# A searched table of due times for the opening part of a fused attention and feed-forward kernel

## The chip, the cores and the metric

One core of one Trainium2 chip runs the program. TensorE (PE; its weight loads appear as PEld), VectorE (DVE), ScalarE (ACT), GpSimd (POOL) and SyncE (SP, which here only issues DMAs) each work through their own instruction list in order and wait for one another by semaphores. The metric is the device time of one execution in microseconds (us).

## The reference

Causal attention over 8 batches, 8 heads, 576 tokens of 64 channels, followed by a feed-forward layer:

```
scores = q @ k^T / 8
heads 0..3: keep key s for query t where 0 <= t - s < 32        (local)
heads 4..7: keep key s <= t where s % 32 == t % 32              (strided)
attn = softmax(scores) @ v ;  x = attn as 4608 tokens x 512
out = gelu(x @ w_in) @ w_out          (w_in 512 x 2048, w_out 2048 x 512)
```

## The kernel before

The 4608 tokens are cut into 9 tiles (`t`) of 512 tokens, and the 2048 hidden channels into 16 slices (`f`) of 128. One **pass** is one `f` of one tile: `H` is 12 matmuls of x with a slice of w_in into a PSUM bank, ACT then computes gelu and the copy `gh` (lines 767, 768), DVE the remainder `gl` (line 770), and `O` is 12 matmuls with a slice of w_out (line 779; H is line 741). Every fp32 operand is held as a high part and a low part, so each product takes three matmuls. TensorE's list is fixed: H of pass n, then O of pass n-1, then H of n+1, and so on. In tile 0 the slices f0 and f1 are done in two half passes each (pass numbers n = 0 to 3), so f2 is pass 4 and f15 is pass 17; H of pass 18 is the first of tile 1. Between passes the fixed list has the local scores of the next tile, `S` (line 425, behind f4 in tile 0), and its local values, `V` (line 466, behind the O of f12).

What the other engines do for this:

- **Weights**, once per f, all in tile 0: `load` (SP, 1 MB), then `lead` (ACT, line 332), `ws` (ACT, 333), `or` (DVE, 335), `hi` (ACT or DVE, 344) and `lo` (line 349, POOL for f > 2, DVE for f0 to f2). H of f needs hi and lo.
- **Local heads**: S on TensorE, `max` on DVE (485), `exp` on ACT (492), `quo` (504), `tr` (transpose, DVE 508), then V. For tile 1 on, `send` (SP, line 455) copies the transposed pieces, 4 pieces of 8 DMAs, ahead of V.
- **Strided heads**: products on POOL (and DVE at the start), sums on DVE, exp on ACT; names `oq`/`ov` for the first two tiles' rows, `q`/`v` later. `xl`, `xs` are x's local and strided halves, each split into h and l.

The order on every engine comes out of a list scheduler in the kernel, `Plan`: each step (`Op`) has candidate engines with a guessed duration and a due time, either given (`fixed`) or worked back from the step's users in `latest`; whenever an engine is free in the plan, the ready step with the earliest due time goes next. The plan's times are not on the chip: only the resulting order of each engine, and its choice of engine, are. The 17 slots of tag `w` hold weights and the opening's data in turn; a load waits until its slot is free.

Of the kernel before, what the change touches and what calls it, by code (L numbers as in the profile page):

```python
# [86 lines left out]
class Op:  # L87
    def __init__(self, eng, fn, deps, due, bufs, table, kb, name, rel, port, fixed):
        self.eng, self.fn, self.deps, self.due, self.bufs = eng, fn, deps, due, bufs
        self.table, self.kb, self.name, self.rel = table, kb, name, rel  # L90
        self.start = self.end = self.last = None
        self.port, self.fixed = port, fixed


class Plan:
# [19 lines left out]
    def run(self, busy):  # L115
        free = dict(busy)
# [7 lines left out]
        nxt, now, state, dma = 0, 0.0, "e", 0.0  # L124
# [33 lines left out]
        port = 0.0  # L158
        h_end = 0.0
        while count < len(self.ops):  # L160
            moved = False
            for e in free:
                if free[e] > now + 1e-9:
                    continue
                best = None
                for op in waiting[e]:
                    if at[op] > now + 1e-9:
                        continue
                    if e == "PE" and op not in self.floating and op is not self.pe[nxt]:
                        continue  # L170
                    if best is not None and op.due >= best.due:
# [73 lines left out]
def attn_ffn_kernel(ctx: ExitStack, tc: tile.TileContext, qk, qk0, vl, vl0, q0, k0, v0, q1, k1, v1, qs, ks, vs, w, out):  # L245
# [54 lines left out]
    def gps(n):  # L300
        return 0.33 + n * 0.00205
# [15 lines left out]
    def weights(f):  # L317
# [33 lines left out]
        o5 = plan.add({"POOL": 2.4} if f > HALVES else {"DVE": 1.25}, lo, [o4], due - 2, [raw, wt], name=f"lo{f}", port=True)  # L351
# [27 lines left out]
    def local(t):  # L379
# [26 lines left out]
        for j in range(NJ):  # L406
# [22 lines left out]
            s_ops[t, j] = plan.add({"PE": 0.4}, score if t else score0, [ld[j]], 0, [lq] + sb[j], name=f"S{t}.{j}")  # L429
# [4 lines left out]
        def after(o, pt, j, due):  # L434
            if t == 0:
# [10 lines left out]
                v_ops[t, j] = plan.add({"PE": 0.65}, value, [o, vo[j // 2]], 0, [vb, pt] + xb[j // 2], name=f"V{t}.{j}")  # L446
            else:
# [8 lines left out]
                o = plan.add({"SP": 4.4}, send, [o], due, [pt, bt], kb=1400, name=f"send{t}.{j}")  # L456
# [12 lines left out]
                v_ops[t, j] = plan.add({"PE": 0.45}, value, [o, vo], 0, [vb, bt] + xb, name=f"V{t}.{j}")  # L469

        for j in range(NJ):
# [37 lines left out]
            o = plan.add({"DVE": 0.7}, first, pair, due - 3, [pt, both] + sb[j], name=f"max{t}.{j}")  # L509
            o = plan.add({"ACT": 1.4}, second, [o], due - 2.5, [pt, both], table="e", name=f"exp{t}.{j}")  # L510
# [41 lines left out]
    def finish(t, sc, shape, deps, due, name):  # L552
# [58 lines left out]
    def unit(t, u, b, r0, nr, row, due):  # L611
# [33 lines left out]
        for i in range(nr):  # L645
# [11 lines left out]
            om = times(n * D, mul, [o, vlo], due - 2, [vb, sc, p], f"pv{name}.{i}")  # L657
# [65 lines left out]
    def ffn(t, wts):  # L723
# [4 lines left out]
        for f, c0, c1 in todo:  # L728
# [5 lines left out]
            MM = N / 2400.0 + 0.0127  # L734
# [222 lines left out]
```

## Time and profile before

| what | value |
|---|---|
| device time, 3 runs | median 881.13 us (880.54 to 881.37) |
| profiled execution | 880.88 us, span 879.0 us (1.9 us lie outside the span) |
| TensorE matmul busy | 838.0 us, 95% of the span |
| ACT, DVE, POOL busy | 410.1, 443.1, 503.4 us |
| mean granted TensorE clock | 0.991 of full speed |

Busy times are of the profiled execution; waits are read from the times at which instructions start.

### The profile page before, as it was taken

The numbers are of one execution on the slowest core, as the hardware profiler recorded it, in microseconds if no ns is written. First come the engines' busy times: TensorE is split into PE (matmuls) and PEld (weight loads), VectorE is DVE, ScalarE is ACT, GpSimd is POOL, SyncE is SP. The second block draws the span as 40 slices with busy tenths as digits, with TensorE's granted clock in tenths as the row PEclk, the third lists the DMA queues.
The fourth block names the chain that finished last, engine by engine and source line by source line (L and its number), as shares of the span: only waits on it lengthen the run. The fifth ranks groups of instructions, "written<-read, shape, count | busy, mean of one in ns | idle before, by whom it ended". The sixth has DMA issues, their size and how long they took to land.

```text
span 879.0 us, 15285 instructions
## 1 busy us (share of the span) xinstructions
PE 838.0 (95%) x5878; PEld 690.5 (79%) x5878; DVE 443.1 (50%) x946; ACT 410.1 (47%) x868; POOL 503.4 (57%) x433
## 2 busy tenths in 40 slices
PE   2798978999999999999999999999999999999997
PEld 1686756888888888888888888888888888888886
DVE  5877746755564655455545547356465651121111
ACT  4789934644454435434553346335623363222222
POOL 2567878876666874865576759477387760000000
PEclk9999988999999999999999999999999999999999
DMA  9928133110330113012211211111210310000001
GB/s 346 385 79 332 60 122 91 58 45 3 120 116 22 48 61 125 24 49 88 86 31 53 88 48 63 59 66 70 101 48 1 109 51 23 1 37 12 1 1 48
DMA packets 27672, 69.67 MB, mean 79 GB/s; under 512 B 5968, under 2 KB 14160, under 8 KB 25296
## 3 DMA queue, kind: packets, MB, share of 16 engines
q1 hardware_dynamic: 27600, 68.70, 22.0%
q8 instruction: 46, 0.75, 0.3%
q14 instruction: 26, 0.21, 0.1%
HBM read 55.05 MB, written 9.44 MB: 73 GB/s over the span
## 4 chain that ended last, share of the span: by engine, by line
PE 84%; ACT 6%; DMA 4%; DVE 2%; SPq 2%; issue 1%; POOL 0%; ACTq 0%
PE banks L741 41%; PE banks L779 40%; DMA w_raw<-in_w_dram 3%; PE banks L466 2%; DVE w_raw L335 2%; SPq L455 2%; ACT lead L332 1%; PE banks L425 1%; ACT w_raw L333 1%; DMA w_kv<-in_v_dram 1%; ACT pt L492 1%; ACT w_wt L344 1%; ACT L492 1%; ACT L767 1%; ACT banks L767 1%
## 5 line engine op out<-in xcount | busy, mean ns | idle before, releaser
L779 PE MATMUL banks<-w_wt,gh 128*128 128x512 f32 x1152 | 355.0, 389 | 0.3 <-ACT gh L768 0.3
L767 ACT ACTIVATE banks<-banks 128x512 f32<-128x512 f32 (+1 forms) x146 | 84.2, 577 | 386.6 <-PE banks L741 386.2
L779 PEld LDWEIGHTS banks<-w_wt,gh 128*128 128x128 f32 x1152 | 216.2, 188 | 45.3 <-ACT gh L768 0.7
L770 DVE TENSOR_TENSOR gl<-banks,gh 128x512 fp32r<-128x512 f32 (+1 forms) x146 | 99.5, 682 | 277.9 <-ACT gh L768 275.5
L779 PE MATMUL banks<-w_wt,gl 128*128 128x512 f32 x576 | 224.4, 390 | 0.8 <-DVE gl L770 0.8
L741 PE MATMUL banks<-xsh,w_wt 128*128 128x512 f32 (+1 forms) x584 | 162.5, 398 | 12.3 <-ACT w_wt L344 5.4
L741 PE MATMUL banks<-xlh,w_wt 128*128 128x512 f32 (+1 forms) x584 | 157.8, 391 | 0.6 <-ACT xlh L366 0.6
L741 PEld LDWEIGHTS banks<-xsh,w_wt 128*128 128x128 f32 x584 | 109.2, 191 | 38.0 <-POOL w_wt L349 6.8
L741 PEld LDWEIGHTS banks<-xlh,w_wt 128*128 128x128 f32 x584 | 111.1, 191 | 23.7 <-ACT xlh L366 0.8
L779 PEld LDWEIGHTS banks<-w_wt,gl 128*128 128x128 f32 x576 | 108.1, 188 | 24.0 <-DVE gl L770 1.7
L741 PE MATMUL banks<-xsl,w_wt 128*128 128x512 f32 (+1 forms) x292 | 91.1, 392 | 0.0
L741 PE MATMUL banks<-xll,w_wt 128*128 128x512 f32 (+1 forms) x292 | 90.5, 389 | 0.0
L768 ACT CAST gh<-banks 128x512 fp32r<-128x512 f32 (+1 forms) x146 | 84.9, 581 | 4.6
L741 PEld LDWEIGHTS banks<-xsl,w_wt 128*128 128x128 f32 x292 | 55.8, 192 | 11.6
L741 PEld LDWEIGHTS banks<-xll,w_wt 128*128 128x128 f32 x292 | 55.4, 190 | 11.6 <-DVE xll L371 0.2
L767 ACT ACT_TABLE_LOAD x38 | 48.8, 1283 | 0.7
L492 ACT ACTIVATE pt<-pt,lsm 128x64 f32<-128x64 f32 x128 | 42.8, 336 | 5.0 <-DVE lsm L485 4.8
L349 POOL TENSOR_TENSOR w_wt<-w_raw,w_wt 128x1024 fp32r<-128x1024 f32 x13 | 32.1, 2472 | 21.1 <-ACT w_wt L344 11.6
L504 POOL TENSOR_TENSOR pt<-pt,lsm 128x256 f32<-128x256 f32 x32 | 21.0, 676 | 26.1 <-DVE lsm L500 12.2
L335 DVE SCALAR_TENSOR_TENSOR w_raw<-w_raw 128x1024 uint32<-128x1024 uint32 x16 | 31.1, 1952 | 4.1 <-ACT w_raw L333 3.8
L585 ACT ACT_TABLE_LOAD x24 | 30.8, 1283 | 0.4
L466 PEld LDWEIGHTS banks<-bt,lq_v 64*64 64x64 f32 x1024 | 20.2, 134 | 7.1 <-issue 3.9
(900 smaller groups left out, 1026.1 us busy)
## 6 DMA issues: line engine op xcount, KB each, us to landing
w_raw<-in_w_dram SPq DMA_DIRECT2D x16, 1023.8 KB, 11.8
lq_qk<-in_qk_dram SPq DMA_DIRECT2D x8, 1280.0 KB, 5.9
lq_v<-in_vl_dram SPq DMA_DIRECT2D x8, 1024.0 KB, 5.2
out_dram<-w_ob SPq DMA_DIRECT2D x24, 256.0 KB, 2.3
sk<-in_ks_dram SPq DMA_DIRECT2D x8, 576.0 KB, 3.8
sv<-in_vs_dram SPq DMA_DIRECT2D x8, 576.0 KB, 3.9
bt<-pt SPq DMA_DIRECT2D x256, 16.0 KB, 1.8
sq<-in_qs_dram SPq DMA_DIRECT2D x8, 448.0 KB, 4.5
```

The lines of the kernel that those rows point to most:

```text
L335: o3 = plan.add({"DVE": 1.25}, lambda e: V.scalar_tensor_tensor(views["word"], views["word"], 13, views["other"], ALU.logical_shift_right, ...
L349: (V if e == "DVE" else G).tensor_tensor(views["t"][:, 1, :], views["word"].bitcast(F32), views["t"][:, 0, :].bitcast(F32), ALU.subtract)
L455: nc.sync.dma_start(bv[d:d + QB, a, :], pv[quarter(g), c, :])
L466: nc.tensor.matmul(xb[b]()[half(i), c:c + QB], vv[half(b), a, 2 * r + i, :], bv[half(b), a, 2 * r + i, :], start=True, stop=True, tile_pos ...
L492: A.activation(pv[:, :, h, :], pt()[:, 256 + h * 64:256 + (h + 1) * 64].rearrange("p (c t) -> p c t", c=2), AF.Exp, bias=sm[0]()[:, h:h + ...
L504: (V if e == "DVE" else G).tensor_tensor(pv, pv, sm[2]().unsqueeze(1).unsqueeze(3).to_broadcast([P, 2, HL, QB]), ALU.mult)
L585: o = plan.add({"ACT": act(n * c)}, lambda e: A.activation(view(), view(), AF.Exp, scale=SC), [o], due - 0.4, [sc], table="e", name=f"sexp ...
L741: nc.tensor.matmul(hp()[:, 0:c1 - c0], w1[f][:, lw, c, :], rx, start=((c, part) == (2, 0)), stop=((c, part) == end))
L767: A.activation(hp()[:, 0:N], hp()[:, 0:N], AF.Gelu)
L768: A.copy(a_()[:, 0:N], hp()[:, 0:N])
L770: o3 = plan.add({"DVE": dve(N)}, lambda e, hp=hp, a_=a_, b_=b_, N=N: V.tensor_tensor(b_()[:, 0:N], hp()[:, 0:N], a_()[:, 0:N].bitcast(F32) ...
L779: nc.tensor.matmul(o, x()[:, sl], w2[f][:, y, :], start=(f == 0 and i == 0), stop=(f == NF - 1 and i == 2))
```

## The change

A table `ORDER` of some 500 entries is added, one per named step of the opening and of the first tiles. For a step in it the due time is replaced by the table's, and a letter behind the number (V, A, G for DVE, ACT, POOL) also fixes the engine. The table was found by a search over the kernel's own scheduler. The scheduler's guessed durations and latencies are replaced by others, `lo` and `quo` may go to either POOL or DVE, gelu and gl get an earlier due time (`urgent`), and from planned time 140 on a step is not started on ACT or DVE just ahead of an expected gelu or gl. TensorE's list and the arithmetic stay as they were.

```diff
+URGENT = 20.0, 100.0
+STEADY = 140.0
+ORDER = """
+qk00:13.89 qk01:25.62 vl00:158.2 vl01:161.77 max0.0:-4534.87 exp0.0:-2303.89 max0.1:-4558.19
...
-    LAT = 0.08
+    LAT = 0.05
+    PE_LAT = 0.2
+    LAP = 0.05
...
         for op in reversed(self.ops):
-            op.due = op.due if op.fixed else latest(op)
+            op.due = op.due if op.fixed else round(latest(op) - op.urgent, 2)
+            if op.name in self.given:
+                op.due, e = self.given[op.name]
+                if e in op.eng:
+                    op.eng = {e: op.eng[e]}
...
+                    if now > self.steady and op.urgent == 0.0:
+                        if e == "ACT" and now - 0.19 < h_end < now + op.eng[e] - 0.5 + (
+                                1.3 * ((op.table == "e") + (state == "g")) if op.table or state == "e" else 0.0):
+                            continue
+                        if e == "DVE" and now - 0.04 < g_end < now + op.eng[e] - 0.4:
+                            continue
...
-                    dma = max(dma, now + 1.6) + op.kb / 370.0
-                    op.end = dma + 1.0
+                    dma = max(dma, now + 1.6) + op.kb / (230.0 if sent < 512 else 120.0 if sent < 1024 else 410.0)
+                    sent += op.kb
+                    op.end = max(dma + 0.6, free[e] + 1.2)
...
-        o5 = plan.add({"POOL": 2.4} if f > HALVES else {"DVE": 1.25}, lo, [o4], due - 2, [raw, wt], name=f"lo{f}", port=True)
+        o5 = plan.add({"POOL": 2.45, "DVE": 1.25}, lo, [o4], due - 2, [raw, wt], name=f"lo{f}", port=True)
...
-                o = plan.add({"SP": 4.4}, send, [o], due, [pt, bt], kb=1400, name=f"send{t}.{j}")
+                o = plan.add({"SP": 4.95}, send, [o], due, [pt, bt], kb=128, name=f"send{t}.{j}")
...
+            o2.urgent = o3.urgent = URGENT[n > 24]
...
+    plan.steady = STEADY
+    for x in ORDER.split():
+        name, due = x.split(":")
+        e = {"V": "DVE", "A": "ACT", "G": "POOL"}.get(due[-1])
+        plan.given[name] = float(due[:-1] if e else due), e
     todo = plan.run({"PE": 1.0, "DVE": 0.3, "ACT": 1.5, "POOL": 3.0, "SP": 0.0})
```

What it does to the lists, at three places. First SP, the first twelve loads (`q01`, `kv0`: strided inputs, `qk0`, `vl0`: the two halves of the local inputs, `raw0`, `raw1`: weights of f0 and f1). Before:

```order
L833 DMA w_q01_140<-in_q0_dram 128x512
L833 DMA w_kv0_142<-in_k0_dram 128x512
L386 DMA lq_qk0_144<-in_qk0_dram 128x1024
L325 DMA w_raw0_146<-in_w_dram 128x4095
L833 DMA w_kv0_142<-in_v0_dram 128x512
L397 DMA w_vl0_149<-in_vl0_dram 128x1024
L833 DMA w_q01_140<-in_q0_dram 128x512
L833 DMA w_kv0_142<-in_k0_dram 128x512
L386 DMA lq_qk0_144<-in_qk0_dram 128x1024
L325 DMA w_raw1_160<-in_w_dram 128x4095
L833 DMA w_kv0_142<-in_v0_dram 128x512
L397 DMA w_vl0_149<-in_vl0_dram 128x1024
```

The same place on SP after the change:

```order
L921 DMA w_kv0_140<-in_k0_dram 128x512
L473 DMA lq_qk0_142<-in_qk0_dram 128x1024
L921 DMA w_q01_144<-in_q0_dram 128x512
L473 DMA lq_qk0_142<-in_qk0_dram 128x1024
L921 DMA w_kv0_140<-in_k0_dram 128x512
L921 DMA w_q01_144<-in_q0_dram 128x512
L484 DMA w_vl0_149<-in_vl0_dram 128x1024
L412 DMA w_raw0_155<-in_w_dram 128x4095
L484 DMA w_vl0_149<-in_vl0_dram 128x1024
L921 DMA w_kv0_140<-in_v0_dram 128x512
L412 DMA w_raw1_159<-in_w_dram 128x4095
L921 DMA w_kv0_140<-in_v0_dram 128x512
```

The second half of qk0 has moved from ninth to fourth, and raw0 from fourth to eighth. Behind these stood raw2, the inputs k1, q1, v1 of the strided part of tile 1, raw3, raw4, qk1 (the local input of tile 1) and raw5; now raw2, q1, v1, k1, qk1, raw3, raw4, raw5. The lists of POOL then have the products oq1.0.0, oq1.0.1 and oq1.1.1, which read k1, ahead of the lo of f2, and oq1.1.0 behind it.

Second SP again, at the sends of tile 1 (`bt` is what V reads, `pt_1_j` the four transposed pieces). Before:

```order
L325 DMA w_raw12_943<-in_w_dram 128x4095
L325 DMA w_raw13_985<-in_w_dram 128x4095
L325 DMA w_raw14_1032<-in_w_dram 128x4095
L455 DMA bt_1_1053<-pt_1_0_732 32x128 x8
L455 DMA bt_1_1053<-pt_1_1_740 32x128 x8
L455 DMA bt_1_1053<-pt_1_2_763 32x128 x8
L455 DMA bt_1_1053<-pt_1_3_769 32x128 x8
L325 DMA w_raw15_1232<-in_w_dram 128x4095
```

The same place after the change:

```order
L412 DMA w_raw12_935<-in_w_dram 128x4095
L542 DMA bt_1_966<-pt_1_0_734 32x128 x8
L412 DMA w_raw13_1011<-in_w_dram 128x4095
L542 DMA bt_1_966<-pt_1_1_743 32x128 x8
L412 DMA w_raw14_1067<-in_w_dram 128x4095
L412 DMA w_raw15_1084<-in_w_dram 128x4095
L542 DMA bt_1_966<-pt_1_2_748 32x128 x8
L542 DMA bt_1_966<-pt_1_3_761 32x128 x8
```

raw15 has moved ahead of the last two sends, and raw13 and raw14 behind the first and the second.

Third DVE, from the gl of pass 9 (f7) to that of pass 10. Before:

```order
L770 TENSOR_TENSOR gl_9_909<-banks_71,gh_9_887 128x512
L638 TENSOR_REDUCE sc_2.0_871<-prod_q2.0.3_884 128x8
L638 TENSOR_REDUCE sc_2.0_871<-prod_q2.0.2_911 128x7
L638 TENSOR_REDUCE sc_2.0_871<-prod_q2.0.1_919 128x6
L770 TENSOR_TENSOR gl_10_939<-banks_71,gh_10_935 128x512
```

The same place after the change:

```order
L857 TENSOR_TENSOR gl_9_873<-banks_71,gh_9_858 128x512
L798 TENSOR_REDUCE w_acc1_820<-prod_ovo1.0.1_850 128x4x64
L422 SCALAR_TENSOR_TENSOR w_raw9_769<-w_raw9_769 128x1024
L798 TENSOR_REDUCE w_acc1_820<-prod_ovo1.0.0_877 128x4x64
L682 STREAM_TRANSPOSE w_acc1_820<-w_acc1_820 128x512
L431 CAST w_wt9_918<-w_raw9_769 128x1024
L587 RECIPROCAL lsm_1_0_735<-lsm_1_0_735 128x8
L436 TENSOR_TENSOR w_wt9_918<-w_raw9_769,w_wt9_918 128x1024
L591 TENSOR_TENSOR pt_1_0_734<-pt_1_0_734,lsm_1_0_735 128x256
L422 SCALAR_TENSOR_TENSOR w_raw10_797<-w_raw10_797 128x1024
L857 TENSOR_TENSOR gl_10_953<-banks_71,gh_10_925 128x512
```

DVE now has the lo of f9 here (L436), which stood on POOL; over the whole tile DVE has 13 of the 16 lo steps, where it had 3, and POOL has those of f2, f6 and f7. The strided work of tile 2 (prod_q2) has moved behind. On ACT the order of exp steps changes too: up to H of pass 18 its list has 12 table loads in place of 16, and behind it 92 in place of 60, since most exp steps of a tile now stand one by one between two gelus.

## Rows read from the trace of the kernel before

**Rows 1.** The page's first line: the span.
```profile
span 879.0 us, 15285 instructions
```
**Rows 2.** Windows: stretch, its us, each engine's busy us, granted clock, DMA share, GB/s.
```profile
0.00:10.00 10.00, 2.60 (x126) 2.32 (x126) 3.13 (x13) 1.49 (x2) 1.75 (x14) 1.00 0.78 252
10.00:40.00 30.00, 15.66 (x274) 13.60 (x275) 24.58 (x72) 23.44 (x62) 16.57 (x16) 1.00 1.02 424
90.00:100.00 10.00, 10.00 (x46) 8.19 (x45) 6.84 (x8) 9.90 (x19) 8.76 (x7) 1.00 0.30 106
120.00:130.00 10.00, 8.75 (x40) 6.74 (x40) 2.76 (x3) 2.85 (x4) 4.06 (x2) 0.68 0.64 241
150.00:200.00 50.00, 50.00 (x342) 41.26 (x342) 29.60 (x78) 27.34 (x68) 39.63 (x38) 1.00 0.22 63
```
**Rows 3.** Timeline of PE: start, us, instruction, count, idle time before and its releaser.
```profile
25.49 1.20 PE L741 MATMUL banks<-xsh,w_wt 128*128 128x256 f32 x4 [2.44 <-ACT w_pt L492]
...
47.78 1.07 PE L741 MATMUL banks<-xsh,w_wt 128*128 128x512 f32 x4
...
58.75 1.49 PE L425 MATMUL banks<-lq_qk 64*32 64x64 f32 x128
...
114.71 2.07 PE L466 MATMUL banks<-bt,lq_v 64*64 64x32 f32 x100
...
136.91 1.65 PE L741 MATMUL banks<-xsh,w_wt 128*128 128x512 f32 x3 [1.69 <-POOL w_wt L349]
...
143.70 1.07 PE L741 MATMUL banks<-xsh,w_wt 128*128 128x512 f32 x4
...
149.14 1.07 PE L741 MATMUL banks<-xsh,w_wt 128*128 128x512 f32 x4
...
221.63 2.53 PE L466 MATMUL banks<-bt,lq_v 64*64 64x32 f32 x128
```
**Rows 4.** Timeline of SP: the four sends of tile 1, and the load behind them.
```profile
98.66 21.56 SPq L455 DMA_DIRECT2D bt<-pt  x32
120.33 0.52 SPq L325 DMA_DIRECT2D w_raw<-in_w_dram  x1
```
**Rows 5.** Timeline of PE and ACT: first users of qk0's second half and of raw1.
```profile
15.79 1.13 PE L413 MATMUL banks<-lq_qk 64*64 64x64 f32 x32 [6.03 <-DMA lq_qk<-in_qk_dram]
18.22 1.11 ACT L332 CAST lead<-w_raw 128x1024 f16<-128x1024 bf16 x1 [2.06 <-DMA w_raw<-in_w_dram]
```
**Rows 6.** The tile w_raw: line, engine, count, duration in ns (min/median/max), first and last start.
```profile
L332 ACT CAST lead<-w_raw x16: 1073/1123/1203, 11.4 to 128.2; 128x1024 f16<-128x1024 bf16 x16
L333 ACT ACTIVATE w_raw<-lead x16: 1107/1131/1172, 12.5 to 129.3; 128x1024 int32<-128x1024 int16 x16
L335 DVE SCALAR_TENSOR_TENSOR w_raw<-w_raw x16: 1175/1662/3455, 13.7 to 130.5; 128x1024 uint32<-128x1024 uint32 x16
L349 POOL TENSOR_TENSOR w_wt<-w_raw,w_wt x13: 2403/2438/2894, 44.7 to 134.5; 128x1024 fp32r<-128x1024 f32 x13
L349 DVE TENSOR_TENSOR w_wt<-w_raw,w_wt x3: 1211/1219/1225, 16.1 to 43.6; 128x1024 fp32r<-128x1024 f32 x3
```
**Rows 7.** Timeline of DVE: an or that ran beside a lo on POOL.
```profile
44.77 3.46 DVE L335 SCALAR_TENSOR_TENSOR w_raw<-w_raw 128x1024 uint32<-128x1024 uint32 x1
```
**Rows 8.** The page's DMA issues: KB each, us to landing.
```profile
bt<-pt SPq DMA_DIRECT2D x256, 16.0 KB, 1.8
```
**Rows 9.** Timeline of ACT: the table load between exp and gelu, a gelu, its copy.
```profile
169.98 1.28 ACT L767 ACT_TABLE_LOAD   x1
171.27 0.58 ACT L767 ACTIVATE banks<-banks 128x512 f32<-128x512 f32 x1
171.88 0.59 ACT L768 CAST gh<-banks 128x512 fp32r<-128x512 f32 x1
```
**Rows 10.** The page's groups: gl, and the exp instructions, count, busy us, mean ns.
```profile
L770 DVE TENSOR_TENSOR gl<-banks,gh 128x512 fp32r<-128x512 f32 (+1 forms) x146 | 99.5, 682 | 277.9 <-ACT gh L768 275.5
L492 ACT ACTIVATE pt<-pt,lsm 128x64 f32<-128x64 f32 x128 | 42.8, 336 | 5.0 <-DVE lsm L485 4.8
```

More of the change, by code (lines that the diff above doesn't have):

```diff
@@ L36, in order_of_rows @@
+sq3.1.3:289.03 smax3.1:274.63
+"""
 def order_of_rows(nb, nr):
@@ L103, in __init__ @@
         self.floating = set()
+        self.given = {}
+        self.steady = 1e9
     def add(self, eng, fn, deps=(), due=0.0, bufs=(), table=None, kb=0, name="", rel=None, port=False, fixed=False):
@@ L123, in run @@
         waiting = {e: [] for e in free}
-        nxt, now, state, dma = 0, 0.0, "e", 0.0
+        nxt, now, state, dma, sent = 0, 0.0, "e", 0.0, 0.0
         after = dict(zip(self.pe, self.pe[1:]))
@@ L145, in offer @@
         def offer(op):
-            at[op] = max([d.end + self.LAT for d in op.deps] + [op.rel])
+            at[op] = max([d.end + (self.PE_LAT if d.engine == "PE" else self.LAT) for d in op.deps] + [op.rel])
             for e in op.eng:
@@ L158, in run @@
         port = 0.0
-        h_end = 0.0
+        h_end = g_end = 0.0
         while count < len(self.ops):
@@ L199, in run @@
                 op.start, op.engine = now, e
-                free[e] = now + dur
                 op.end = now + dur
+                free[e] = op.end - (self.LAP if e in ("DVE", "ACT", "POOL") else 0.0)
                 if op.port and e in ("DVE", "POOL"):
@@ L207, in run @@
                         h_end = op.end
+                if op.table == "g":
+                    g_end = op.end
                 if op.kb:
-                    dma = max(dma, now + 1.6) + op.kb / 370.0
-                    op.end = dma + 1.0
+                    dma = max(dma, now + 1.6) + op.kb / (230.0 if sent < 512 else 120.0 if sent < 1024 else 410.0)
+                    sent += op.kb
+                    op.end = max(dma + 0.6, free[e] + 1.2)
                 tick += 1
@@ L508, in fifth @@
                 V.transpose(pt()[:, 256:512], pt()[:, 0:256])
-            o = plan.add({"DVE": 0.7}, first, pair, due - 3, [pt, both] + sb[j], name=f"max{t}.{j}")
-            o = plan.add({"ACT": 1.4}, second, [o], due - 2.5, [pt, both], table="e", name=f"exp{t}.{j}")
+            o = plan.add({"DVE": 0.66}, first, pair, due - 3, [pt, both] + sb[j], name=f"max{t}.{j}")
+            o = plan.add({"ACT": 1.37}, second, [o], due - 2.5, [pt, both], table="e", name=f"exp{t}.{j}")
             exps.append((o, fourth, fifth, pt, j, due))
@@ L516, in local @@
             for o, fourth, fifth, pt, j, due in exps:
-                o = plan.add({"POOL": 0.75} if t else {"POOL": 0.75, "DVE": 0.46}, fourth, [rec], due - 1.5, [pt, both], name=f"quo{t}.{j}", port=True)
+                o = plan.add({"POOL": 0.65, "DVE": 0.46} if t < 2 else {"POOL": 0.65}, fourth, [rec], due - 1.5, [pt, both], name=f"quo{t}.{j}", port=True)
                 o = plan.add({"DVE": 0.46}, fifth, [o], due - 1, [pt], name=f"tr{t}.{j}")
@@ L579, in seventh @@
             (V if e == "DVE" else G).tensor_tensor(view(), view(), wide(m()[:, 16:16 + n]), ALU.mult)
-        mul = {"POOL": 0.33 + 0.0021 * n * c}
+        mul = {"POOL": 0.2 + 0.0015 * n * c}
         if t < 2:
             mul["DVE"] = 0.25
-        o = plan.add({"DVE": 0.24}, first, deps, due - 0.6, [sc, m], name=f"smax{name}")
+        o = plan.add({"DVE": 0.2}, first, deps, due - 0.6, [sc, m], name=f"smax{name}")
         o = plan.add(mul, second, [o], due - 0.5, [sc, m], name=f"ssub{name}", port=True)
@@ L586, in finish @@
                      table="e", name=f"sexp{name}")
-        o = plan.add({"DVE": 0.24}, fourth, [o], due - 0.3, [sc, m], name=f"ssum{name}")
+        o = plan.add({"DVE": 0.2}, fourth, [o], due - 0.3, [sc, m], name=f"ssum{name}")
         o = plan.add({"ACT": 0.23}, fifth, [o], due - 0.2, [m], name=f"seps{name}")
-        o = plan.add({"DVE": 0.2}, sixth, [o], due - 0.1, [m], name=f"srec{name}")
+        o = plan.add({"DVE": 0.18}, sixth, [o], due - 0.1, [m], name=f"srec{name}")
         return plan.add(mul, seventh, [o], due, [sc, m], name=f"squo{name}", port=True)
@@ L605, in turn @@
         xops.setdefault((t, "s"), []).append(split(src, dst, X[t][1], [tr], [o,
-            *([xops[t - 1, "s"][0][0]] if t else [])], due, n, f"xs{name}", {"POOL": gps(n)} if t > 1 else {"POOL": gps(n), "DVE": dve(n)}))
+            *([xops[t - 1, "s"][0][0]] if t else [])], due, n, f"xs{name}", {"POOL": 0.22 + 0.00205 * n} if t > 1 else {"POOL": 0.22 + 0.00205 * n, "DVE": dve(n)}))
     bload = {}
@@ L656, in add @@
                                 AX.X, ALU.add)
-            om = times(n * D, mul, [o, vlo], due - 2, [vb, sc, p], f"pv{name}.{i}")
+            om = times(n * D, mul, [o, vlo], due - 2, [vb, sc, p, acc], f"pv{name}.{i}")
             outs.append(plan.add({"DVE": dve(n * D)}, add, [om], due - 2, [p, acc], name=f"sv{name}.{i}"))
```

78 lines of the change are left out of this document (70 added, 8 removed).

## The prediction, made before the change was run

> **What bounds the kernel now.** I read the windows of the whole span first, then the timeline of TensorE, then at each place where it stands still the timeline of the engine that releases it. The span is 879.0 us [rows 1], and the profiled execution took 880.88 us, 0.25 us under the median of the runs; all sums below are made against 880.9. From 150 us on TensorE is busy in every microsecond [rows 2], and the stream runs like that to the end, so the steady part can't gain. What can gain lies ahead of H of pass 18, at 143.7 us [rows 3]. A pass costs 149.14 - 143.70 = 5.44 us there; an S costs about 1.5 us and an undisturbed V 2.5 us [rows 3].
>
> Three stretches lose time against that rate. In the opening the first H starts at 25.5 us and H of f3 (pass 5) only at 47.8 us.
>
> From f3 to V: H of f3 to H of f13 and the O of f2 to that of f12 are eleven passes, 11 x 5.44 = 59.8 us, and S 1.5; they took 114.7 - 47.8 = 66.9 us, so 5.6 us are lost. ACT is full there, 9.90 of 10 us [rows 2].
>
> From V to pass 18: V and two passes need 2.5 + 10.9 = 13.4 us and took 143.7 - 114.7 = 29.0 us, so 15.6 us are lost. The 32 sends kept SP for 21.6 us from 98.7, V waited for the last of them, and raw15, queued behind them, was issued at 120.3 [rows 4]; H of f15 got its lo at 136.9 [rows 3]. After the wait at V the granted clock fell, to a mean of 0.68 in 120 to 130 us [rows 2], which is a mixture of its two levels, 2.4 and 1.2 GHz; that loss is part of the 15.6.
>
> **The change, part by part.**
>
> *Opening.* What a load waits for: 2.52 MB came in the first 10 us and 0.424 MB per us after [rows 2]. qk0's second half was ninth, with 3.93 MB up to its end, which passes at 13.3 us; its user ran at 15.8. raw1 ended at 4.98 MB, 15.8 us; its user ran at 18.2 [rows 5]. So a load is of use some 2.4 us after its bytes have passed in order. By that rule the new list gives: raw1 (5.50 MB) 19.4 us, k1 (9.44 MB) 28.7, raw3 (11.80 MB) 34.3; qk0's second half (1.57 MB) lands before 12.4 in place of 15.8. So V of all of tile 0 comes ahead of the first H, and not half of it behind.
>
> The first H then hangs on ACT: lead and ws of f1, 1.1 us each from 19.4 [rows 6], stand ahead of xs, a cast of 0.6 and its remainder on DVE, some 0.7: about 23.3 us, 2.2 earlier. f3 is bound by two chains. By load: raw3 at 34.3, then lead 1.1, ws 1.1, or 1.2, hi 1.1 (as a lead, the same width), lo 1.2 [rows 6] gives 40.0, the least possible. By POOL: k1 at 28.7, then oq1.0.0 (768 wide, three quarters of the 2.4 of a 1024 wide lo on POOL), oq1.0.1, oq1.1.1 and lo of f2, 1.8 + 3 x 2.4 = 9.0, and a DVE step of 0.7 that comes between. The row where or took 3.46 in place of 1.18 beside a lo of POOL [rows 6, 7] shows why: the two don't run at once, the later one waits for the whole of the other. So lo of f2 ends at 38.4; or of f3, ready at 36.5, follows to 39.6, oq1.1.0 takes its turn to 41.4 while ACT does hi, and lo of f3 ends at 42.6. TensorE's own path is shorter: 23.3 plus about 14 for the four half passes and f2. I take 42.6 for H of f3, 5.2 us earlier than 47.8. Bounds: 40.0 (no such wait at all) and 47.4 (two more turns of POOL).
>
> *f3 to V.* Up to pass 18 ACT loses 4 table loads of 1.28 us [rows 9], 5 us in all, so it is no longer full. lo costs 1.2 on DVE against 2.4 on POOL [rows 6], so each weight is ready sooner once its hi is done. The price is on DVE: it had 6.84 busy us in 90 to 100 [rows 2], and 1.84 passes in 10 us bring 1.84 x 1.2 = 2.2 more: about 9.0 of 10. That holds only because POOL, at 8.76 of 10, loses 1.84 x 2.4 = 4.4 us there, so that DVE finds it idle more often. Bounds for what is still lost: 0, and 13 us if every added lo from f8 to f14 (seven) had to wait for a full POOL step of 2.4 and delayed TensorE in full (17, less 3.5 of spare, below). I take 1 us, by the sum of 9.0, and gain 4.6.
>
> *V to pass 18.* Four sends in 21.6 us make 5.4 each [rows 4]. Now only two stand behind raw15. With 1 us lost H of f12 starts at 42.6 + 9 x 5.44 + 1.5 + 1 = 94.1. Pieces 2 and 3 are transposed on DVE just ahead of the gl of f11, some 92.5 us; two sends and 1.8 to land [rows 8] give 105.1, and TensorE gets to V at 94.1 + 10.9 = 105.0. raw15 waits for the slot of raw11, free after its lo near 88 us; even a landing as late as 100 and the five weight steps, 5.8 us, are ready before H of f15 is due at 94.1 + 3 x 5.44 + 2.5 = 112.9. I take 0.5 us lost (0 to 3: piece 3 a POOL step late), so 15.1 gained, the fallen clock included.
>
> *Steady part.* It costs 32 table loads more on ACT, 41 us. What hides them: one exp step between two gelus makes 2 x 1.28 + 4 x 0.34 + 1.2 (gelu and copy) = 5.1 us of ACT [rows 9, 10], inside a pass of 5.44. Beyond it stands a spare: TensorE wants a gelu's result only a pass later, 5.44 less gelu's 1.2 and gl's 0.7 [rows 10], so 3.5 us. I take 0, at most 3.
>
> Here a rule of the Trainium skill speaks against the change. ACT_TABLE_LOAD takes 1.28 us and gelu starts 0.01 us after it ends [rows 9]; nothing else stands between. ScalarE: Activation LUTs, What ACT_TABLE_LOAD costs, puts a switch at 2.66 us, the load and about 1.38 us of drain; by that the steady part would overflow (last rival).
>
> The sum: 5.2 + 4.6 + 15.1 = 24.9, 880.9 - 24.9 = **856 us**.
>
> **Rivals.** The forecast, 850.5 to 863 us, has 62%.
>
> DVE becomes the bound between f8 and V. For it: 9.0 of 10 is close, lists are in order, so one or that waits for POOL holds the gl and lo behind it. Price: 7 to 13 us lost there instead of 1, 863 to 868 us, and with f3 late by two POOL turns up to 873. Against: POOL's share falls. 22%.
>
> TensorE alone bounds the opening: f3 at about 37.5 and nothing lost later, 143.7 - (37.5 + 74.7) = 31.5 gained, 849 us, where 74.7 are thirteen passes, S and V. For it: loads may land sooner with less beside them. Against: raw3's chain to 40.0. 9%.
>
> Slower, by the steady part. In each of some 32 intervals an exp step now stands alone on ACT with its gelu behind it. If the max that exp reads is held on DVE behind POOL, gelu is late. An interval must slip by 0.3 + 3.5 us before TensorE sees it, and by 24.9 / 32 = 0.8 more in every one to cancel the gain; beyond that the kernel is slower. If each of the two table switches cost twice the row's 1.28, an interval would take 7.7 us, 2.3 over the pass: 32 x 2.3 less a spare of 3.5 in each of seven tiles is 49 us lost, 905 us. Against: TensorE never waited in 150 to 200 [rows 2], where ACT switched tables as well, and after a run of such intervals ACT has passes with a gelu alone to recover in. 5%. By the Trainium skill, ScalarE: Activation LUTs, What ACT_TABLE_LOAD costs, the interval is 2 x 2.66 + 2.6 = 7.9 and the time some 911 us, an estimate from that page; the rows of this trace speak against it.
>
> The table doesn't do what it says: the planned order meets other waits, and the new lists stall as long as the old ones elsewhere, 879 to 883 us: 2%.
>
> **How the numbers follow.** The predicted time is that of the forecast's sum. The range 850 to 870 us holds nearly all of the forecast and most of the DVE rival, about 80%; below it is TensorE alone, above it the rest. Its ends are also those of the bounds: 40.0 for f3 with nothing lost later makes 850.8, and 47.4 with 5 us of DVE and 2 of V lost makes 867. A measurement of this kernel can tell about 0.2%, 1.8 us, from no change. Faster by more: the first three cases together, 93%; within it 2%; slower 5%.
>
> **What would show each step.** In the profile after: H of f3 at 40 to 45 us, with raw3's lead near 34 and lo of f2 on POOL ending near 38; waits of TensorE for DVE and ACT between f3 and V of 0 to 3 us in total; sends 2 and 3 after raw15, V waiting under 2 us; H of pass 18 near 119; the granted clock at 1.00 from there on; no waits of TensorE after it. I am wrong if f3 starts after 47, if TensorE waits several times for lo or gl on DVE around f9 to f12, if raw14 or raw15 land late behind the sends in front of them, or if steady passes show waits for gelu.

## The result, and the profile after

The changed kernel took 856.58 us (856.29 to 856.78, 4 runs) against 880.84 (879.05 to 881.37, 4 runs) for the kernel before in the same series: ratio 0.9728, interval 0.9711 to 0.9745, 24.3 us faster. Predicted were 856.0 us, 850 to 870. The profiled execution took 856.75 us, its span is 854.6; the span before was 879.0 [rows 1], so the traces have 24.4 us to account for.

TensorE's timeline, the rows that answer to [rows 3]:

```profile
22.27 1.22 PE L828 MATMUL banks<-xsh,w_wt 128*128 128x256 f32 x4 [4.42 <-ACT xsh L453]
...
41.88 0.96 PE L828 MATMUL banks<-xsh,w_wt 128*128 128x512 f32 x3 [1.04 <-DVE w_wt L436]
...
47.23 1.07 PE L828 MATMUL banks<-xsh,w_wt 128*128 128x512 f32 x4
...
77.57 0.97 PE L828 MATMUL banks<-xsh,w_wt 128*128 128x512 f32 x3 [1.07 <-DVE w_wt L436]
...
93.82 1.07 PE L828 MATMUL banks<-xsh,w_wt 128*128 128x512 f32 x4
...
100.46 0.97 PE L828 MATMUL banks<-xsh,w_wt 128*128 128x512 f32 x3 [0.76 <-DVE w_wt L436]
...
105.90 2.63 PE L553 MATMUL banks<-bt,lq_v 64*64 64x32 f32 x128
...
114.04 1.07 PE L828 MATMUL banks<-xsh,w_wt 128*128 128x512 f32 x4
...
119.48 1.07 PE L828 MATMUL banks<-xsh,w_wt 128*128 128x512 f32 x4
```

H of f3 is broken by a wait of 1.04 us for its lo. H of f4 is not, and starts at 47.23, so f3 counts as 47.23 - 5.44 = 41.8. V stands in one piece of 2.63 us, without the waits for sends. H of f15 (114.04) has no wait, and H of pass 18 starts at 119.48. Term by term:

| stretch | before | after | gained | predicted |
|---|---|---|---|---|
| up to H of f3 | 47.8 | 41.8 | 6.0 | 5.2 |
| f3 to V | 66.9 | 105.9 - 41.8 = 64.1 | 2.8 | 4.6 |
| V to pass 18 | 29.0 | 119.5 - 105.9 = 13.6 | 15.4 | 15.1 |
| pass 18 to the end of the span | 879.0 - 143.7 = 735.3 | 854.6 - 119.5 = 735.1 | 0.2 | 0 |

Windows as in [rows 2], with one more, 80 to 90 us, in which f10 and its neighbours run, and then all waits of TensorE from 40 us to the end (line waited for, us in total, times, longest):

```profile
80.00:90.00 10.00, 10.00 (x46) 8.29 (x45) 9.70 (x14) 9.71 (x18) 4.74 (x3) 1.00 0.28 95
...
90.00:100.00 10.00, 9.70 (x43) 7.66 (x41) 6.40 (x10) 7.49 (x9) 4.38 (x6) 1.00 0.74 260
...
120.00:130.00 10.00, 10.00 (x46) 8.29 (x45) 5.76 (x11) 5.55 (x10) 6.86 (x6) 1.00 0.38 89
...
150.00:200.00 50.00, 50.00 (x339) 41.48 (x337) 27.02 (x50) 27.47 (x55) 38.17 (x36) 1.00 0.08 23
```
```profile
PE banks L828 <- DVE w_wt L436: 2.9, 3, 1.1
```

In 120 to 130 us the granted clock is 1.00 where it was 0.68. GpSimd is busy for 4.38 of 10 us in 90 to 100 where it was for 8.76. From 40 us on, three waits for a lo on VectorE, of f3, f9 and f13, are all that TensorE still waits for.

### The profile page after: what moved, and what is told of

The parts are those of the page before. It is cut to its first block, busy times and chain, and to the rows that moved or that the text cites. A ratio compares the mean times of both kernels' runs of the same rounds, so it can differ in the third digit from the quotient of the medians.

```text
span 854.6 us, 15282 instructions
## 1 busy us (share of the span) xinstructions
PE 830.8 (97%) x5878; PEld 687.0 (80%) x5878; DVE 451.3 (53%) x959; ACT 444.4 (52%) x889; POOL 483.8 (57%) x427
## 4 chain that ended last, share of the span: by engine, by line
PE 91%; DMA 4%; ACT 2%; DVE 1%; SPq 1%; issue 1%
PE banks L828 44%; PE banks L867 43%; DMA w_raw<-in_w_dram 3%; PE banks L553 2%; PE banks L512 1%; DMA w_kv<-in_v_dram 1%; SPq L542 1%; ACT pt L579 0%; DVE w_raw L422 0%; DVE w_wt L436 0%; ACT w_raw L420 0%; SPq L921 0%; SPq L484 0%; ACT L854 0%; ACT L579 0%
## 5 line engine op out<-in xcount | busy, mean ns | idle before, releaser
L828 PE MATMUL banks<-xsh,w_wt 128*128 128x512 f32 (+1 forms) x584 | 159.1, 392 | 8.6 <-ACT xsh L453 4.4
L828 PE MATMUL banks<-xlh,w_wt 128*128 128x512 f32 (+1 forms) x584 | 156.0, 388 | 0.0
L422 DVE SCALAR_TENSOR_TENSOR w_raw<-w_raw 128x1024 uint32<-128x1024 uint32 x16 | 24.7, 1546 | 3.2 <-ACT w_raw L420 3.2
L572 DVE CUSTOM_DVE_ANT_0 pt<-banks,mask 128x64 f32<-128x64 f32 x128 | 20.4, 220 | 7.9 <-PE banks L512 5.7
```

The costliest lines, as they stand in the source:

```text
L422: o3 = plan.add({"DVE": 1.25}, lambda e: V.scalar_tensor_tensor(views["word"], views["word"], 13, views["other"], ALU.logical_shift_right, ...
L572: V.tensor_tensor_reduce(pt()[:, 256 + h * 64:256 + (h + 1) * 64], sb[j][h % 2]()[:, c + h // 2 * 64:c + (h // 2 + 1) * 64], masks[0 if t ...
L828: nc.tensor.matmul(hp()[:, 0:c1 - c0], w1[f][:, lw, c, :], rx, start=((c, part) == (2, 0)), stop=((c, part) == end))
```

## The experiments

Where an edit below sets `start`, it changes the plan's time of one step after planning, by which the lists are sorted: that step alone changes its place. The median of the kernel before lay between 880.59 and 881.47 us in all series, so times are also compared with the 856.58 across series. Where an experiment adds work, its heading says so.

**1. The rules without the table** (`e1_rules_no_table`).

```diff
-ORDER = """qk00:13.89 ..."""
+ORDER = ""
```

> The changed kernel with an empty table: the new guesses and rules alone order the lists. SP then has the twelve first loads as before the change, and raw15 ahead of all four sends. Theory (the opening and the move of raw15 are two separate gains): the opening stays as before, H of f3 near 47.8 us, so its 6.0 us are not gained, while raw15's part is: of the 15.6 us lost between V and pass 18 before, the two waits of f15, 4.63 + 1.69 = 6.3, go, and perhaps some of the fallen clock; 866 to 875 us, 871 taken. Rival 1 (the table does nearly all): 877 to 882. Rival 2 (the rules do nearly all): 855 to 860.

Measured: 870.66 us (870.0 to 871.73), ratio 0.9875 (0.9859 to 0.9892). TensorE and SP (source lines lie lower by some 65 without the table):

```profile
47.29 1.43 PE L763 MATMUL banks<-xsh,w_wt 128*128 128x512 f32 x4
...
117.74 0.83 PE L488 MATMUL banks<-bt,lq_v 64*64 64x32 f32 x16 [2.09 <-DMA bt<-pt]
```
```profile
98.67 20.97 SPq L477 DMA_DIRECT2D bt<-pt  x32
```

f3 starts at 47.29: 0.5 us of the opening is gained. raw15 stands ahead of the sends, so f15 doesn't wait, but the sends start at 98.67 as before and V waits 4.1 us for them in three pieces; from V to H of pass 18 the trace has 134.80 - 113.62 = 21.2 us, where the changed kernel has 13.6. The new guesses and rules make 10.4 of the 24.3 us, and the table the rest.

**2. raw15 early in the kernel before** (`e2_before_raw15_early`).

```diff
+    for o in plan.ops:
+        if o.name in ("send1.1", "send1.2", "send1.3"):
+            o.deps.append(load_of[15])
     todo = plan.run(...)
```

> The kernel before, with one rule added: the sends 1 to 3 come behind the load of raw15, so that raw15 is issued near 104 us in place of 120.3. Theory (raw15 behind the sends and V's wait for the last send are two losses that add up): f15's waits of 4.63 and 1.69 us go, V still waits for the last send near 121, so 880.9 - 6.3 = 874.6, or up to 3 us less if the clock falls for a shorter time: 871 to 876. Rival (V's wait and the clock that falls after it hold the loss, and raw15 is hidden behind them): 878 to 881.

Measured: 871.32 us (870.13 to 873.01), ratio 0.9887 (0.987 to 0.9903). SP, and the waits of TensorE for sends from 40 us on:

```profile
103.71 0.53 SPq L325 DMA_DIRECT2D w_raw<-in_w_dram  x1
104.33 16.48 SPq L455 DMA_DIRECT2D bt<-pt  x24
```
```profile
PE banks L466 <- DMA bt<-pt: 2.2, 2, 2.0
```

raw15 leaves SP 16.6 us sooner, the waits of f15 are gone, and the time falls by 9.8 us with V still waiting. That is more than the 6.3 of those waits. H of f13 now waits 2.85 us for its hi and lo, so V is reached at 117.32, 2.6 later than before; V's own wait falls from 3.9 to 2.2, and the granted clock in 120 to 130 us is 0.83 where it was 0.68. From V to H of pass 18 it is 135.13 - 117.32 = 17.8 us in place of 29.0. So the place of raw15 is worth, by the whole time, about two thirds of the term from V to pass 18; that the sends' own place is the rest isn't shown by this run.

**3. raw15 late in the changed kernel** (`e3_after_raw15_late`).

```diff
+    at["send1.2"].start = at["load15"].start + 1.5
+    at["send1.3"].start = at["load15"].start + 2.0
+    at["load15"].start = at["lead15"].start - 0.01
```

> The changed kernel with one move on SP: raw15 stands behind the sends 2 and 3, as before the change, all else in the changed order. The sends then end near 104.8 us, raw15 lands near 110 and its lead, which stands ahead of the gelu of f13 on ScalarE, holds that gelu by some 7 us; the lo of f15 ends near 124 in place of 113.2. Theory (the place of raw15 among the sends makes most of the gain between V and pass 18): 8 to 14 us slower than the changed kernel, 865 to 871, with the granted clock below 1.00 behind the wait. Rival (the gain there comes from the rest of the order): 856 to 859.

Measured: 867.09 us (866.7 to 867.39), 10.5 us slower than the changed kernel. SP, TensorE, VectorE and ScalarE:

```profile
105.52 0.51 SPq L412 DMA_DIRECT2D w_raw<-in_w_dram  x1
```
```profile
117.14 1.65 PE L828 MATMUL banks<-xsh,w_wt 128*128 128x512 f32 x3 [7.20 <-DVE w_wt L436]
```
```profile
113.27 0.19 DVE L657 TENSOR_REDUCE ssm_2.0_1090<-sc_2.0_932 128x4 f32<-128x32 f32 x1 [9.53 <-ACT sc_2.0_932 L672]
...
114.46 2.62 DVE L436 TENSOR_TENSOR w_wt<-w_raw,w_wt 128x1024 fp32r<-128x1024 f32 x1
```
```profile
110.61 1.09 ACT L419 CAST lead<-w_raw 128x1024 f16<-128x1024 bf16 x1 [8.87 <-DMA w_raw<-in_w_dram]
```

The wait of 7.20 us isn't at the O of f13, as expected, but one H earlier, at f14. raw15 holds its lead on ScalarE for 8.87 us, an exp of the strided heads stands behind that lead, a sum on VectorE waits 9.53 us for the exp, and the lo of f14 stands behind the sum. The price and the theory hold; the place was one step off. The mean granted clock in 100 to 120 us is 0.79.

**4. lo on GpSimd in the changed kernel** (`e4_lo_on_pool`).

```diff
+    for o in todo:
+        if o.name in [f"lo{f}" for f in range(8, 16)]:
+            o.engine = "POOL"
```

> The changed kernel with the lo of f8 to f15 on GpSimd at the same places of the order, 2.45 us each in place of 1.2 on VectorE. Theory (lo on VectorE makes each weight ready sooner and costs VectorE nothing that counts): the waits of f9 and f13, 1.07 and 0.76 us, grow by 1.2 to 2.5 us each and one to three more appear, 2 to 8 us slower than the changed kernel, 858 to 865. Rival (VectorE is near its bound between f8 and V, as the second case of the prediction had it): the waits of f9 and f13 shrink, 854 to 856.

Measured: 857.27 us (856.69 to 857.59), 0.7 us slower, which is within the 0.2%: between theory and rival. The waits from 40 us on:

```profile
PE banks L828 <- POOL w_wt L436: 1.2, 3, 0.5
PE banks L828 <- DVE w_wt L436: 1.0, 1, 1.0
PE banks L828 <- POOL sc_2.0_932 L712: 0.6, 1, 0.6
```

The wait of 1.0 us is that of f3, as before. Where two waits of 1.07 and 0.76 stood, four now stand, of 0.64 (f9, put down to another step of GpSimd), 0.19, 0.42 and 0.54 (f13): 1.8 us in all, as much as the two made. In this order either engine carries the lo steps.

**5. qk0's second half late** (`e5_qk0_late`).

```diff
+    at["qk01"].start = at["vl01"].start + 0.01
```

> The changed kernel with one move on SP: the second half of qk0 stands behind both halves of vl0 and raw0 again, ninth in the list. By the opening's rule its bytes then end at 4.19 MB, 13.9 us, and it is of use at 16.3 in place of 9.09. Theory (the place of this load sets the opening): the scores and exp steps of the second half, which stand ahead of the weight steps on ScalarE, come 7 us later, the first H near 28.5 and H of f3 at 45 to 48 in place of 41.8: 860 to 864. Rival (f3 hangs on raw3 and on GpSimd's chain from k1, which don't move): H of f3 at 41 to 43.5, 856 to 858.

Measured: 862.89 us (861.99 to 863.93), 6.3 slower than the changed kernel. TensorE:

```profile
15.08 1.13 PE L500 MATMUL banks<-lq_qk 64*64 64x64 f32 x32 [8.00 <-DMA lq_qk<-in_qk_dram]
...
27.55 1.22 PE L828 MATMUL banks<-xsh,w_wt 128*128 128x256 f32 x4 [4.41 <-ACT xsh L453]
...
47.72 1.07 PE L828 MATMUL banks<-xsh,w_wt 128*128 128x512 f32 x4
```

One load moved by five places puts f3 at 47.72, where it was before the change (47.78, [rows 3]), although raw3 and k1 keep their places and k1 is used at 28.13. What comes late with the scores are the steps of the lists: two products of GpSimd wait 2.36 and 1.82 us for VectorE, the lead of f3 runs at 40.30 in place of 33.84, behind a gelu, and the lo of f3 ends at 47.23. The granted clock, 0.94 in 10 to 40 us where it was 1.00, has a part in it. The opposite run, this one load moved forward in the kernel before, was not made.

**6. v1 later, lo of f9 earlier** (`e6_v1_late_lo9`): an attempt at a faster version.

```diff
+    at["v1r"].start = at["load3"].start + 0.01
+    at["qk1"].start = at["load4"].start + 0.01
+    at["lo9"].start = at["rec1.1"].start - 0.01
```

> The changed kernel with two moves. On SP v1 and qk1 come behind raw3 and raw4, so that k1 is usable 2.4 us earlier, raw3 5 us earlier; on VectorE the lo of f9 comes ahead of a reciprocal for which VectorE stood idle 0.81 us. Theory (f3 waits by raw3 and by GpSimd's chain from k1; f9 waits by that one place in VectorE's list): the waits of f3 (1.04) and f9 (1.07) go, 2 to 2.5 us faster than the changed kernel, 854.0 to 855.0. Rival (another step is late next, in ScalarE's or VectorE's order): one or both waits stay, 855.5 to 857.

Measured: 857.79 us (856.79 to 858.14): not faster. GpSimd, VectorE and TensorE:

```profile
25.93 1.82 POOL L773 TENSOR_TENSOR prod_oqo1.0.0_446<-w_q,w_k 128x768 f32<-128x768 f32 x1 [5.51 <-DMA w_k<-in_k_dram]
```
```profile
26.21 2.62 DVE L436 TENSOR_TENSOR w_wt<-w_raw,w_wt 128x1024 fp32r<-128x1024 f32 x1
```
```profile
42.15 1.07 PE L828 MATMUL banks<-xsh,w_wt 128*128 128x512 f32 x4
```

The waits of f3 and f9 are gone or under 0.3 us, and f9 to f10 is 0.6 us shorter; f13 still waits, 0.4 and 0.8 us. But k1 came 2.6 us earlier, and its first product now lies over the lo of f1 on VectorE, which takes 2.62 in place of 1.22 us; the second half pass is late and f3 starts at 42.15, later than 41.8. The rival's reason holds, another step is late next; the time lies 0.8 above its range.

**7. Without the rule for the steady part** (`e7_no_steady_rule`).

```diff
-URGENT = 20.0, 100.0
-STEADY = 140.0
+URGENT = 20.0, 0.0
+STEADY = 1e9
```

> The changed kernel without the rule that keeps ScalarE and VectorE clear ahead of a gelu or gl from planned time 140 on, and without the larger lead of gelu and gl in the due times there. Theory (the steady part has spare in any order): 856 to 858, TensorE waits under 1 us behind pass 18. Rival (that rule keeps gelu in time now that exp steps stand between gelus): TensorE waits for gelu in several passes, 860 to 870.

Measured: 856.18 us (855.9 to 856.41), no difference; TensorE waits 2.3 us in all from 40 us on, none of it behind pass 18. The theory holds: the steady part has spare in either order.

**8. Two table loads in every pass** (`e8_switch_each_pass`). It adds an exp whose result nothing reads.

```diff
                 A.copy(a_()[:, 0:N], hp()[:, 0:N])
+                if n > 40:
+                    A.activation(dust, warm, AF.Exp)
```

> The changed kernel with one more exp, of 128x1 elements, behind the copy of every pass from 41 on, so that each of some 105 passes holds at least two table loads; 139 table loads more in all. Theory (a switch costs the 1.28 us of the load and no more, and a gelu may be some 3.5 us late): ScalarE had 2.6 us of work per pass in 200 to 600 us and gets 139 x 1.28 / 105 = 1.7 and the exp's 0.2 more, 4.5 of 5.44; 856 to 862, with a few waits for gelu where local exp steps stand. Rival (a switch costs twice that, 1.3 us more): 7.1 of 5.44, some 1.7 us more in each pass, over 1000 us.

Measured: 857.21 us (856.51 to 857.86), 0.6 us over the changed kernel. ScalarE in one pass:

```profile
500.90 0.59 ACT L855 CAST gh<-banks 128x512 fp32r<-128x512 f32 x1
501.50 1.28 ACT L857 ACT_TABLE_LOAD   x1
502.79 0.20 ACT L857 ACTIVATE dust<-warm 128x1 f32<-128x1 f32 x1
503.01 1.28 ACT L854 ACT_TABLE_LOAD   x1
507.38 0.58 ACT L854 ACTIVATE banks<-banks 128x512 f32<-128x512 f32 x1 [3.08 <-PE banks L828]
```

139 loads more cost TensorE next to nothing. The gaps around the two loads ahead of the wait are 0.01 and 0.02 us: here a switch is the load and no more. And gelu's table is loaded at 503.01 although gelu itself waits for TensorE until 507.38. A switch of twice the load's time would have filled each pass and made over 1000 us by the expectation's sum. So the prediction's rival of a slower steady part falls. The Trainium skill, ScalarE: Activation LUTs, What ACT_TABLE_LOAD costs, adds some 1.38 us of drain to a switch. None of it shows in these gaps.

**9. Four table loads put back among the exp steps of tile 1** (`e9_four_loads_back`). It adds two gelus whose results nothing reads.

```diff
             def second(e, pt=pt, sm=sm, j=j):
+                if t == 1 and j in (0, 3):
+                    A.activation(dust, masks[0][:, 0:1], AF.Gelu)
```

> The changed kernel, in whose block of three exp steps at 69.4 to 75.4 us a gelu of 128x1 elements stands ahead of the second and of the third, so that ScalarE does four table loads more there: the four that the order saved, 4 x 1.28 + 2 x 0.2 = 5.5 us. Theory (the gain between f3 and V comes from exp steps that share a table, since ScalarE is full there): the gelu at 76.69 comes at 82.2, TensorE wants it and its gl by 80.2, so it waits some 3.5 us, and the weight steps behind it are late too: 3 to 5 us slower than the changed kernel, 859.5 to 862. Rival (ScalarE has room there and the gain comes from VectorE's order): under 1 us slower, 856.3 to 857.6.

Measured: 862.09 us (861.54 to 862.75), 5.5 slower. TensorE, VectorE, and the window behind the wait:

```profile
82.00 1.65 PE L831 MATMUL banks<-xsh,w_wt 128*128 128x512 f32 x3 [6.11 <-DVE w_wt L436]
```
```profile
80.65 0.20 DVE L590 RECIPROCAL lsm<-lsm 128x8 f32<-128x8 f32 x1 [6.67 <-ACT lsm L587]
80.77 1.17 DVE L436 TENSOR_TENSOR w_wt<-w_raw,w_wt 128x1024 fp32r<-128x1024 f32 x1
```
```profile
80.00:90.00 10.00, 8.00 (x23) 6.37 (x24) 8.66 (x12) 9.56 (x16) 5.86 (x4) 0.66 0.04 10
```

The price is that of the theory, the way is another: TensorE waits for no gelu, but for the lo of f9, which stands on VectorE behind a reciprocal that needs the last exp step. VectorE stood idle for 6.67 us with the lo ready to run.

**10. lo on VectorE in the kernel before** (`e10_before_lo_dve`).

```diff
+    for o in todo:
+        if o.name in [f"lo{f}" for f in range(8, 16)]:
+            o.engine = "DVE"
```

> The kernel before with the lo of f8 to f15 on VectorE at the same places of the order. Theory (the engine of lo is worth under 1 us, as the opposite move in the changed kernel said; the order of the steps ahead of it holds it): 879 to 882. Rival (lo on VectorE was worth the larger part of the 4.6 us that the prediction gave to this stretch): 875 to 878.

Measured: 880.43 us (878.12 to 883.1), ratio 0.9995 (0.9983 to 1.0008): no difference. TensorE, H of f3 and V:

```profile
46.73 1.07 PE L741 MATMUL banks<-xsh,w_wt 128*128 128x512 f32 x4
...
112.74 1.77 PE L466 MATMUL banks<-bt,lq_v 64*64 64x32 f32 x84
```

H of f3 to V took 112.74 - 46.73 = 66.0 us in its trace, 0.9 less than before, and V then waited 4.7 us for the sends, which stayed where they were; so the stretch, and not the time, is what tells here.

**11. Three moves undone at once** (`e11_three_undone`): the edits of 3, 5 and 9 together.

> The changed kernel with three moves undone at once: qk0's second half ninth on SP (alone 862.89 - 856.58 = 6.3 us), raw15 behind the sends 2 and 3 (alone 867.09 - 856.58 = 10.5), four table loads more among the exp steps of tile 1 (alone 862.09 - 856.58 = 5.5). Theory (three separate losses of TensorE, one behind the other, that make up nearly all of the gain of 24.3): they add up, 856.6 + 22.3 = 878.9, taken as 877 to 881. Rival (they overlap, a later wait absorbs an earlier one): 868 to 875.

Measured: 877.30 us (876.57 to 878.31), 20.7 us slower than the changed kernel. The waits from 40 us on:

```profile
PE banks L831 <- DVE w_wt L436: 13.0, 2, 6.9
```

The two waits of 6.1 and 6.9 us stand one behind the other, f3 starts at 47.88: the losses, which come to 22.3 us one by one, make 20.7 together. The other 3.6 of the gain are not in these three moves.

**12. Exp steps in pairs in the kernel before** (`e12_before_exp_pairs`).

```diff
+    at["exp1.1"].start = at["exp1.0"].start + 0.01
+    at["exp1.3"].start = at["exp1.2"].start + 0.01
```

> The kernel before with the exp steps of tile 1 in pairs on ScalarE, the second behind the first and the fourth behind the third, so that four table loads (5.1 us) fall away between f5 and V; the rest of the order and the sends stay. Theory (table loads on a full ScalarE hold the weights and gelus between f3 and V): of the 5.6 us lost from f3 to V 2.5 to 4.5 go, TensorE reaches V at 110 to 112.5 in place of 114.7, and since V then waits for the last send near 121 as before, the time hardly moves, 878 to 881. Rival (the order on VectorE and GpSimd holds these passes): V at 113.5 to 115.

Measured: 882.32 us (881.0 to 883.89), ratio 1.0012 (1.0002 to 1.0022). TensorE:

```profile
66.06 1.07 PE L741 MATMUL banks<-xsh,w_wt 128*128 128x512 f32 x4
75.29 1.07 PE L741 MATMUL banks<-xsh,w_wt 128*128 128x512 f32 x4
...
116.63 2.08 PE L466 MATMUL banks<-bt,lq_v 64*64 64x32 f32 x100
```

Four table loads fewer, and V is reached 1.9 us later. The second exp step of the pair now stands ahead of a gelu and of the hi of f7; f6 to f7 takes 9.2 us in place of 6.3. V and the time lie outside the ranges of theory and rival alike. The theory, that the number of table loads holds these passes, falls: here what stood behind the exp steps at that place counted more. What the loads alone are worth isn't shown, since the pairing moves the steps as well.

## Why the prediction was right, and where it was off

*What bounds the kernel* was read rightly. The steady part gained 0.2 us, and all the rest came from ahead of pass 18. That the sum was met so closely, 24.4 us in the traces against 24.9, is in part luck: the four terms are off by +0.8, -1.8, +0.3 and +0.2. Two of the prediction's sums don't come out of its own terms: 40.0 for f3 with nothing lost later gains 7.8 + 5.6 + 15.6 = 29.0 and makes 851.9, not 850.8, and the upper bound makes 866.3, not 867. Neither moves the range.

*Opening* (5.2 predicted, 6.0 measured). The rule for loads, 2.4 us behind their bytes in order, held to 0.5 us: k1 was used at 28.52 (28.7 predicted), the lead of f3 ran at 33.84 (34.3). The chain that was said to set f3 is in these rows of ScalarE, GpSimd and VectorE:

```profile
33.84 1.13 ACT L419 CAST lead<-w_raw 128x1024 f16<-128x1024 bf16 x1 [0.85 <-DMA w_raw<-in_w_dram]
```
```profile
28.52 1.84 POOL L773 TENSOR_TENSOR prod_oqo1.0.0_448<-w_q,w_k 128x768 f32<-128x768 f32 x1 [7.79 <-DMA w_k<-in_k_dram]
...
35.49 2.45 POOL L436 TENSOR_TENSOR w_wt<-w_raw,w_wt 128x1024 fp32r<-128x1024 f32 x1
```
```profile
36.16 2.87 DVE L422 SCALAR_TENSOR_TENSOR w_raw<-w_raw 128x1024 uint32<-128x1024 uint32 x1 [1.32 <-ACT w_raw L420]
...
40.42 1.42 DVE L436 TENSOR_TENSOR w_wt<-w_raw,w_wt 128x1024 fp32r<-128x1024 f32 x1
```

The lo of f2 ended at 37.94 (38.4), the or of f3 waited for it and ended at 39.03 (39.6), and the lo of f3 ended at 41.8 (42.6). The first H came at 22.27 (23.3; the terms given for it add up to 22.9). All of these are off by up to 1 us, and to one side. Further off is TensorE's own path, which was put at about 14 us from the first H to H of f3 and took 40.45 - 22.27 = 18.2: 1.95 in three waits, for the hi and the lo of f1 and for xsl, and some 1.5 in the first H, whose matmuls of 256 columns followed one another at 0.21 us (four from 23.72 to 24.57) against 0.12 from 26.13 on, although the granted clock of 10 to 40 us is given as 1.00. So the chain by GpSimd did come last, but only by the wait of 1.04 us and not by the 5 that the sums had. Experiment 5 shows that the place of one load, put back, undoes the whole term. It does so although the loads of this chain stay: the steps ahead of it in the lists hold it, which the prediction had not among its bounds.

*f3 to V* (4.6 predicted, 2.8 measured). This is the step that was mis-sized: 1 us was taken as still lost, and 2.8 were. Two places make it up: f9 to f10 took 82.94 - 76.11 = 6.8 us (1.4 over a pass) and f13 to V 105.90 - 99.25 = 6.65 (1.2 over). Their rows on VectorE, and one of ScalarE:

```profile
75.41 0.20 DVE L587 RECIPROCAL lsm<-lsm 128x8 f32<-128x8 f32 x1 [0.81 <-ACT lsm L584]
75.53 1.99 DVE L436 TENSOR_TENSOR w_wt<-w_raw,w_wt 128x1024 fp32r<-128x1024 f32 x1
...
96.23 2.19 DVE L422 SCALAR_TENSOR_TENSOR w_raw<-w_raw 128x1024 uint32<-128x1024 uint32 x1 [0.35 <-ACT w_raw L420]
```
```profile
91.43 1.11 ACT L419 CAST lead<-w_raw 128x1024 f16<-128x1024 bf16 x1 [1.53 <-DMA w_raw<-in_w_dram]
```

The first is the lo behind the reciprocal, which itself took 1.99 us in place of 1.2 beside a product on GpSimd. The second is an or that ran beside another such product. By these rows raw13 has a part in it: it went out at 86.38, behind the first send, and its lead waited 1.53 us for it. The lead of f14 waited 0.99 in the same way. Loads late behind the sends in front of them were one of the prediction's signs of being wrong, for raw14 and raw15; here it shows in small, and no run puts raw13 back. The rest is the rival of VectorE and GpSimd: 2.6 us with raw13's part, and not 7 to 13. ScalarE, said to be no longer full, was busy for 9.71 of 10 us in 80 to 90 and 7.49 in 90 to 100; VectorE, put at about 9.0, for 9.70 and 6.40. Of the two reasons given, lo on VectorE (for f8 to f15) is worth under 1 us (experiments 4 and 10). For the saved table loads no gain of their own is shown: put back into the new order they cost 5.5 us, by way of one reciprocal (experiment 9), and taken out of the old one by pairing they gained nothing (experiment 12). Which moves of the order bring the 2.8 us stays open.

*V to pass 18* (15.1 predicted, 15.4 measured). H of f12 started at 93.82 (94.1), V at 105.90 (105.0), and SP was done with the last sends just ahead of it, at 105.83:

```profile
92.05 1.00 SPq L412 DMA_DIRECT2D w_raw<-in_w_dram  x2
94.08 11.75 SPq L542 DMA_DIRECT2D bt<-pt  x16
```

So there was no room left: had TensorE come to V sooner and the sends not, it would have waited for them. raw15 is the second of the two loads and went out near 92.7, not as soon as 88, when its slot was to be free: in SP's list it stood behind the second send, which kept SP from 87.01 to 91.95, and raw14. H of f15 was ready all the same. Experiments 2 and 3 put raw15 at 9.8 and 10.5 us of the whole time. In experiment 1, with raw15 early and the sends as late as before, this stretch took 7.6 us more than in the changed kernel, where the sends start at 80 in place of 98.7; the sends alone were not moved in any run. The clock came with the waits: none over 1.1 us is left behind 40 us, and it stayed at 1.00.

*Steady part* (0 predicted, 0.2 gained). Experiment 8 put 139 table loads more into it for 0.6 us: there was room for them, since a table is loaded while ScalarE would wait anyway. Experiment 7 shows that the order kept clear for gelu and gl wasn't needed for it.

## What to carry to other kernels

Read where the engine that bounds the kernel stands still, and move the one instruction that the late one is queued behind: two loads, put back by a few places, cost 17 of the 24 us. A step that is ready costs its whole delay when it stands behind one that waits, so look at what stands ahead of it in its list before giving it a faster engine. The losses of three moves added up here to within 1.6 us, but of the single moves tried for a gain (experiments 2, 6, 10 and 12) only that of raw15 brought one; experiment 6 brought the next collision forward.

## What the runs showed of the hardware that was not expected

- The table for gelu is loaded as soon as ScalarE gets to it, ahead of gelu's wait for TensorE (503.01 against 507.38 us, experiment 8), so a switch that falls into idle time of ScalarE is hidden. 139 loads of 1.28 us cost 0.6 us in all.
- Behind one wait of 6.11 us (experiment 9) TensorE's granted clock was 0.66 on the mean of 80 to 90 us, a mixture of 2.4 and 1.2 GHz, where it had been 1.00; behind the waits of up to 1.07 us in the changed kernel, from 40 us on, it stayed at 1.00.
- A load that comes earlier can cost time: k1 at 25.93 in place of 28.52 us lengthened a lo on VectorE from 1.22 to 2.62 us (experiment 6).
